# Fewer weight conversions in mid-attention, a row of -1 that stays in its tile, tail values split once per pair of heads

## The chip, the cores and the metric

The kernel runs on one core of one Trainium2 chip. The metric is the device time of one execution in microseconds (us), as the median of the runs shown. Five engines work beside each other on a core: TensorE (PE), VectorE (DVE), ScalarE (ACT), GpSimd (POOL) and SyncE (SP), which issues most of the DMAs.

## What is computed

```python
# 1: attention with rotary position, 4 batches x 8 heads, S = 576, D = 64
q_rot, k_rot = rotate(q), rotate(k)
attn = softmax(q_rot @ k_rot.T / 8)            # sums get +1e-9
x = (attn @ v)  ->  (4, 576, 512)
# 2: gated layer
u, v = split(gelu(x @ w_in));  v = layernorm(v) * g_ln
x = x + (u * (w_sg @ v + b_sg)) @ w_out
# 3: low-rank mixing of tokens, then two channel layers
u = x + (x.T @ U @ V).T
out = u + relu(u @ w_ch1) @ w_ch2
```

The weights w_in, U, V, w_out, w_ch1 and w_ch2 arrive as 64-bit floats in raw bits and are converted on the chip. Products in stages 2 and 3, and the scores, are made from a high and a low part of each number (high = the value rounded by a copy into the fp32r type, low = value minus high), so that three products stand for one.

## The kernel before, in words

**Attention** goes over 32 heads (two heads are a pair, 16 pairs) in slots. A head has five slots, one for each chunk c of its 576 keys (four of 128, a tail of 64). The main loop (lines 436 to 470) writes out by hand the order of all engines: in slot t = 5h + c PE makes the scores of head h, chunk c (`scores`, L244), ACT takes the exponent into a tile `pc` (L247), and three slots later PE multiplies by the values (`values`, L272). About thirteen slots ahead PE makes the same scores the other way round for the row maximum (`row_max`, L215), which DVE reduces (L220). These two kinds of score tile share three PSUM buffers ("ss"). Everything else is hung on a slot with `later(slot, fn)` and issued at the end of that slot; each engine then works through its own list in that order.

What is hung there for a head: the rotation, three POOL operations (`rope`, L147 to L149) at 26, 25 and 23 slots ahead; `high` (ACT copy L161 and one DMA) at 20 ahead; `low` (POOL subtraction L166 and two DMAs) at 17 ahead; and, at 11 ahead, a POOL memset (L172) that writes the row of -1 by which a row maximum is subtracted in the second score product. That row is row 64 of `K2`; `low` writes all 128 rows of `K2` and so wipes it each time. For the tail chunk, exponents are split (ACT L253, DVE `ph` L255) and so are the values: `value_stacks` has one ACT copy (L180) and one subtraction (L181; POOL, and DVE for the first two heads) for each head, in four tiles `VS`.

`finish` (L279 to L335) works once per pair at slot t0 = 10i + 12: the row sums are collected by two SP DMAs into `rc` (L303), at t0 + 5 POOL adds 1e-9 (`guard`, L306), at t0 + 7 DVE takes the reciprocal (L309), SP writes it to DRAM (L312, t0 + 8) and reads it back spread over rows (L317, t0 + 11), and DVE multiplies the two heads (`apply`, L324) at t0 + 24 and t0 + 26.

**Conversions** (`converted`, L337 to L343) are hung in the same slots. A chunk is a DMA into `raw64` (two buffers), 15 slots later ACT L71, DVE L72 to L75 in four successive slots, then an ACT copy (L349) and a POOL subtraction (L350) for the high and low part. There are eleven chunks, ten slots apart: eight of w_in (128 x 512) computed from slots 30, 40 ... 100, U (128 x 160) from 110, two halves of V (128 x 288) from 120 and 130. `t64` has one buffer.

**After attention** PE's order alone is written by hand; a list scheduler with a timeline of its own orders the other engines. The gated layer's first products (`v_step`, weights WVH and WVL) come first, then `u_step` (WUH, WUL), then the mixing by w_sg, whose rows come by DMA into two buffers `g` and are split by ACT (L516) and POOL (L506). Memory of the attention pool is reused by these tiles.

Of the kernel before, what the change touches and what calls it, by code (L numbers as in the profile page):

```python
# [29 lines left out]

LEAD = 26, 25, 23, 20, 17, 11
LEAD_IN = (-20, -19, -19, -8, -8, 1), (-19, -18, -16, -3, -1, 4), (-3, -3, 0, 2, 4, 8)
FIRST = (-17, -10), (-9, -9)

BY_ACT = (0, 1, 1, 1, 1), (1, 1, 0, 1, 1), (1, 0, 1, 1, 1)

LOAD, LOAD_V, SPLIT_V, SPLIT_V_FIRST = 30, 11, (6, 1), (-11, -1)


AHEAD, RAMP_FROM, RAMP, MAX_1, ROW, ROW_0, ROW_1 = 12, -1, 25, -1, 2, -8, -9

INVERSE = 5, 7, 8, 11, (24, 26)

MATRIX, APART, CONVERT, ROWS = 15, 10, 15, (151, 159)


IDLE = 17, 2, 5, 0, 2, 5, 6, 1, 0, 1
# [3 lines left out]
def tile_kernel(ctx: ExitStack, tc: tile.TileContext, qk, vv, tabs, w_in, g_ln, wsgT, b_sg, w_out, u_r, v_r, w1, w2, out):  # L53
# [32 lines left out]
    D = 64  # L86
# [45 lines left out]

    SPLITS = list(range(NC))[SPLIT]
    VSs = [p1.tile([P, 2, len(SPLITS), D + 1], F32R, name=f"VS_{i}") for i in range(4)]

    def load(h):
        nc.sync.dma_start(RAW[h % NR], qk[h // NHEAD, h % NHEAD].rearrange("c p s -> p c s"))
# [14 lines left out]
    def stacks(h, ticks):  # L152

        rot = RAW[h % NR][:, 0]
        K1, Q1, K2, Q2 = (t[h % NS] for t in (K1s, Q1s, K2s, Q2s))
        a, z = slice(0, D), slice(D, P)

        def high():  # L160
            nc.scalar.activation(K1, rot, AF.Copy)  # L161
            both = f(Qs[h % NS][a, :2 * S]).rearrange("p (a s) -> p a s", a=2)
            nc.sync.dma_start(both, f(K1[z]).rearrange("p (a s) -> p a s", a=1).to_broadcast([D, 2, S]))

        def low():
            nc.gpsimd.tensor_tensor(K2, rot, f(K1), ALU.subtract)  # L166
            nc.sync.dma_start(f(Q1[z]), f(K2[z]))
            nc.sync.dma_start(f(K1[z]), f(K1[a]))
        if h < len(BY_ACT):
            steps = rope(nc.gpsimd, h) + first_stacks(h)  # L170
        else:
            steps = rope(nc.gpsimd, h) + (high, low, lambda: nc.gpsimd.memset(f(K2[D:D + 1]), -1.0))  # L172
            value_stacks(h)
        for tick, fn in zip(ticks, steps):
            later(tick, fn)

    def value_stacks(h):
        VS = VSs[h % 4]
        src = VVs[(h // 2) % 3][:, SPLIT, h % 2, :D]
        later(max(NC * h - SPLIT_V[0], SPLIT_V_FIRST[0]), lambda: nc.scalar.activation(VS[:, 0, :, :D], src, AF.Copy))  # L180
        later(max(NC * h - SPLIT_V[1], SPLIT_V_FIRST[1]), lambda: (nc.gpsimd if h > 1 else nc.vector).tensor_tensor(VS[:, 1, :, :D], src, f(VS[:, 0, :, :D]), ALU.subtract))  # L181

    def first_stacks(h):

        rot = RAW[h % NR][:, 0]
        K1, Q1, K2, Q2 = (t[h % NS] for t in (K1s, Q1s, K2s, Q2s))
        a, z = slice(0, D), slice(D, P)

        def copy(on_act, out, x):
            if on_act:  # L190
                nc.scalar.activation(out, x, AF.Copy)  # L191
            else:
                nc.vector.tensor_copy(out, x)

        def high():
            e = BY_ACT[h]
            copy(e[0], Q1[z], rot[z])
            copy(e[1], Q1[a], rot[z])
            copy(e[2], K1[a], rot[a])
            copy(e[3], K1[z], rot[a])  # L200
            copy(e[4], Q2[a, 0:S], rot[z])

        def low():
            nc.vector.tensor_tensor(Q1[z], rot[z], f(Q1[z]), ALU.subtract)
            nc.vector.tensor_tensor(K2[a], rot[a], f(K1[a]), ALU.subtract)
        value_stacks(h)
        return high, low

# [28 lines left out]
    def scores(h, c):  # L237
        kk = TS[c]
        K1, Q1, K2, Q2 = (t[h % NS] for t in (K1s, Q1s, K2s, Q2s))
        ps = psp.tile([P, 2, 512], F32, tag="ss", name=f"st{h}_{c}", bufs=3)  # L240
        for l, r, st in ((K1, Q1, True), (K2[0:D + 1], Q2, False)):
# [12 lines left out]
        PCS[h, c] = ph  # L254
        lows.append(lambda: nc.vector.tensor_tensor(ph[D:], pt, f(ph[:D]), ALU.subtract))  # L255

    def values(h, c, t0):
        if c == 0:
            PVS[h] = psp.tile([P, 2, 512], F32, tag="pv", name=f"pv{h}", bufs=1)
        kk = TS[c]  # L260
        pc = PCS.pop((h, c))
        for n in range(2):
            ns = slice(n * HALF, (n + 1) * HALF)
            o = PVS[h][:D + 1, n, :HALF]
            if c in SPLITS:
# [13 lines left out]
    def finish(h, t0):  # L279
# [73 lines left out]
    def u_chunk(t0):
# [516 lines left out]
def _layout(q, k, v, moe_w_in, moe_g_ln, moe_w_sg, moe_b_sg, moe_w_out, moe2_U, moe2_V, moe2_w_ch1, moe2_w_ch2):  # L870
# [44 lines left out]
```

## Time and profile before

| | |
|---|---|
| median of 3 runs | 956.35 us (955.83 to 956.82) |
| the profiled execution's own time | 957.72 us |
| its span, first to last instruction | 955.9 us |
| mean granted TensorE clock | 0.989 of full speed |
| PE busy | 927.9 us (97%) |
| DVE, ACT, POOL busy | 542.5, 346.8, 409.9 us |

The span is cut into stretches below. A busy PE is not a PE at its peak, since matmuls are pipelined; so the pace in attention is read from the distance between equal events of successive heads. A line number is a line of the kernel before; `x2` means that two instructions are shown as one row.

### The profile page before, as it was taken

The page shows a single profiled execution, that of the slowest core. Times are in us where ns is not written, and L with a number is a line of the kernel's source. Part 1 is how long each engine was busy: PE and PEld are TensorE (multiplying, and loading weights), DVE is VectorE, ACT ScalarE, POOL GpSimd, SP SyncE. Part 2 cuts the span into 40 slices and gives each one's busy share as a digit, 9 for nine tenths or more (in the row PEclk, how much of TensorE's full clock was granted, in tenths as well). Part 3 has the DMA queues.
Part 4 walks back from the last instruction along what each step waited for, and adds up shares of the span by engine and source line. Part 5 has one row for each costly group of instructions (what it writes and reads, how often), then busy time and mean ns, then how long its engine had stood idle before and what let it go on. Part 6 is the DMA issues. An engine that isn't in the chain of part 4 may idle for free.

```text
span 955.9 us, 13163 instructions
## 1 busy us (share of the span) xinstructions
PE 927.9 (97%) x5179; PEld 784.5 (82%) x5180; DVE 542.5 (57%) x721; ACT 346.8 (36%) x550; POOL 409.9 (43%) x352
## 2 busy tenths in 40 slices
PE   5899999999999999999999899999999999999998
PEld 2588777777887888999999787888888888888887
DVE  7766899999874486334338845642642552222222
ACT  4356666666656443313225322311220320101000
POOL 7787999999943485231417533210210220000000
PEclk7899999999999999999999999999999999999999
DMA  5477776776630500000003001320220210000112
GB/s 176 127 206 201 210 206 182 207 191 173 168 90 14 164 25 1 1 1 19 5 23 111 22 23 46 109 67 1 88 88 1 67 45 0 1 1 23 45 48 86
DMA packets 57301, 77.93 MB, mean 82 GB/s; under 512 B 29756, under 2 KB 33111, under 8 KB 57239
## 3 DMA queue, kind: packets, MB, share of 16 engines
q1 hardware_dynamic: 56928, 77.01, 28.7%
q8 instruction: 41, 0.67, 0.3%
q14 instruction: 22, 0.17, 0.1%
q10 hardware_dynamic: 310, 0.08, 0.0%
HBM read 55.02 MB, written 4.79 MB: 63 GB/s over the span
## 4 chain that ended last, share of the span: by engine, by line
PE 74%; DVE 17%; issue 3%; DMA 2%; POOL 2%; ACT 1%; SPq 0%; ACTq 0%; DVEq 0%; POOLq 0%
PE a L542 21%; PE r L542 20%; PE pv L272 10%; PE st L244 6%; PE w L542 5%; DVE MX L220 4%; PE m L542 3%; PE sm L215 3%; PE u L542 3%; PE v L542 3%; DVE ph L255 2%; DVE t L74 1%; DVE t L72 1%; DVE X L324 1%; DVE t L75 1%
## 5 line engine op out<-in xcount | busy, mean ns | idle before, releaser
L272 PE MATMUL pv<-pc,VV 128*65 128x288 f32 x512 | 144.7, 405 | 0.5 <-DVE sums L293 0.5
L220 DVE TENSOR_REDUCE MX<-sm 128x1 f32<-128x576 f32 (+1 forms) x160 | 117.6, 751 | 36.5 <-PE sm L215 33.6
L244 PE MATMUL st<-Q,K 65*128 65x288 f32 (+3 forms) x640 | 126.5, 320 | 1.6 <-DVE MX L220 1.2
L735 DVE SCALAR_TENSOR_TENSOR RL<-r,RH 128x1024 fp32r<-128x1024 f32 (+1 forms) x38 | 42.3, 1112 | 123.8 <-ACT RH L734 123.7
L734 ACT ACTIVATE RH<-r 128x1024 fp32r<-128x1024 f32 (+1 forms) x38 | 35.6, 936 | 207.2 <-PE r L542 207.2
L244 PEld LDWEIGHTS st<-Q,K 65*128 65x128 f32 (+3 forms) x640 | 95.6, 179 | 16.2 <-DVE MX L220 5.4
L750 DVE TENSOR_TENSOR X<-a,X 128x256 f32<-128x256 f32 (+4 forms) x65 | 46.4, 745 | 90.8 <-PE a L542 90.7
L247 ACT ACTIVATE pc<-st 128x576 f32<-128x576 f32 x128 | 82.8, 648 | 36.5 <-PE st L244 31.1
L542 PE MATMUL a<-RH,setB 128*128 128x512 f32 (+1 forms) x320 | 93.3, 368 | 0.0
L272 PEld LDWEIGHTS pv<-pc,VV 128*65 128x65 f32 x512 | 68.5, 136 | 29.5 <-DVE sums L293 0.7
L215 PE MATMUL sm<-K,Q 128*128 128x288 f32 (+1 forms) x320 | 76.8, 325 | 12.8 <-ACT Q L191 6.9
L542 PE MATMUL a<-RH,setA 128*128 128x512 f32 (+1 forms) x288 | 83.8, 367 | 0.0
L542 PE MATMUL r<-UH,setA 128*128 128x512 f32 (+1 forms) x256 | 73.1, 364 | 0.1
L542 PE MATMUL r<-UH,setB 128*128 128x512 f32 (+1 forms) x256 | 73.2, 363 | 0.0
L215 PEld LDWEIGHTS sm<-K,Q 128*128 128x128 f32 (+1 forms) x320 | 52.5, 184 | 20.2 <-ACT Q L191 7.4
L542 PEld LDWEIGHTS a<-RH,setB 128*128 128x128 f32 x320 | 58.2, 189 | 10.0
L506 POOL TENSOR_TENSOR setB<-t,setB 128x512 fp32r<-128x512 f32 x16 | 20.7, 1294 | 102.9 <-ACT setB L695 91.8
L542 PEld LDWEIGHTS a<-RH,setA 128*128 128x128 f32 x288 | 52.1, 188 | 9.0
L542 PE MATMUL a<-RL,setB 128*128 128x512 f32 (+1 forms) x160 | 58.9, 368 | 0.0
L148 POOL TENSOR_TENSOR raw<-raw,tab 128x576 f32<-128x576 f32 x31 | 54.5, 1760 | 5.6 <-DMA raw<-in_qk 5.6
L506 POOL TENSOR_TENSOR setA<-t,setA 128x512 fp32r<-128x512 f32 x16 | 21.5, 1352 | 73.7 <-ACT setA L695 69.9
L542 PEld LDWEIGHTS r<-UH,setA 128*128 128x128 f32 x256 | 46.1, 188 | 8.2 <-DVE X L676 0.4
(170 smaller groups left out, 2030.3 us busy)
## 6 DMA issues: line engine op xcount, KB each, us to landing
raw<-in_qk SPq DMA_DIRECT2D x31, 576.0 KB, 4.8
raw<-in_w SPq DMA_DIRECT2D x24, 512.0 KB, 3.6
Q<-K SPq DMA_DIRECT2D x29, 288.0 KB, 3.5
VV<-in_vv SPq DMA_DIRECT2D x16, 320.0 KB, 3.9
rb<-rr SPq DMA_DIRECT2D x15, 288.0 KB, 3.7
Q<-K SPq DMA_DIRECT2D x29, 144.0 KB, 2.4
K<-K SPq DMA_DIRECT2D x29, 144.0 KB, 2.4
raw<-in_w_in SPq DMA_DIRECT2D x8, 512.0 KB
```

The lines of the kernel that those rows point to most:

```text
L148: lambda: e.tensor_tensor(raw[:, 1], raw[:, 1], tab[:, 1], ALU.mult),
L215: nc.tensor.matmul(ps[:TS[t], n, :HALF], Q1[:, t * P:t * P + TS[t]], K1[:, n * HALF:(n + 1) * HALF], start=True, stop=True)
L220: nc.vector.tensor_reduce(MXs[h % 2][:TS[t], t:t + 1], ps[:TS[t], :, :HALF], AX.XY, ALU.max)
L244: nc.tensor.matmul(ps[:kk, n, :HALF], l[:, c * P:c * P + kk], r[:, ns], start=st, stop=not st)
L247: nc.scalar.activation(h2(pc[:kk]), ps[:kk, :, :HALF], AF.Exp, scale=0.125)
L255: lows.append(lambda: nc.vector.tensor_tensor(ph[D:], pt, f(ph[:D]), ALU.subtract))
L272: nc.tensor.matmul(o, l, r, start=(c == 0 and j == 0), stop=(c == NC - 1 and j == len(pr) - 1))
L506: return nc.gpsimd.tensor_tensor(out, a, b, ALU.subtract)
L542: nc.tensor.matmul(o, l, rr, start=(j == 0), stop=(j == n - 1))
L734: nc.scalar.activation(RH[:, s], ps[:, :, :WIDE[blk]], AF.Relu)
L735: nc.vector.scalar_tensor_tensor(RL[:, s], ps[:, :, :WIDE[blk]], 0.0, f(RH[:, s]), ALU.max, ALU.subtract)
L750: nc.vector.tensor_tensor(X[b][:, e2, xs], ps[:, :n, us], X[b][:, e2, xs], ALU.add)
```

## The change

1. **Conversions.** U from slot 40, the first half of V from 80 and the second from 115; two chunks of w_in from 60 and 100; the other six from 125, 132, 139, 146, 153 and 160. The DMA is issued 8 slots ahead of the first five and 6 slots ahead of the six. The four chunks for `v_step` come before the four for `u_step`.
2. **The row of -1.** Queries and keys change places in the tiles: ACT's copy goes to `Q1`, its DMA to the halves `K1` and `K2` of one tile (64 rows each), POOL's subtraction to `Q2`, whose row 64 is overwritten by the row maximum later in any case. `K2` is 65 rows high; nothing writes its last row after the first time. The memset stays for the first use of each of the five buffers only.
3. **Tail values** are split once per pair (128 columns instead of 64), in two tiles.
4. **The guard** (+1e-9) moves from POOL at t0 + 5 to DVE at t0 + 7, right ahead of the reciprocal.

```diff
-LEAD = 26, 25, 23, 20, 17, 11
+LEAD = 26, 25, 23, 20, 17
-INVERSE = 5, 7, 8, 11, (24, 26)
+INVERSE = 7, 8, 11, (24, 26)
-MATRIX, APART, CONVERT, ROWS = 15, 10, 15, (151, 159)
+MATRIX, SMALL, ROWS = ((60, 8), (100, 8)) + tuple((t, 6) for t in range(125, 165, 7)), ((40, 8), (80, 8), (115, 8)), (151, 159)
...
-    K1s = [p1.tile([P, S], F32R, name=f"K1_{i}") for i in range(NS)]
-    Qs = [p1.tile([P, S + NC * P], F32R, name=f"Q_{i}") for i in range(NS)]
-    Q1s = [t[:, :S] for t in Qs]
-    Q2s = [t[:D + 1, S:] for t in Qs]
-    K2s = [p1.tile([P, S], F32R, name=f"K2_{i}") for i in range(NS)]
+    Q1s = [p1.tile([P, S], F32R, name=f"Q1_{i}") for i in range(NS)]
+    Ks = [p1.tile([P, 2 * S], F32R, name=f"K_{i}") for i in range(NS)]
+    K1s = [t[:, :S] for t in Ks]
+    K2s = [t[:D + 1, S:] for t in Ks]
+    Q2s = [p1.tile([P, NC * P], F32R, name=f"Q2_{i}") for i in range(NS)]
...
         def high():
-            nc.scalar.activation(K1, rot, AF.Copy)
-            both = f(Qs[h % NS][a, :2 * S]).rearrange("p (a s) -> p a s", a=2)
-            nc.sync.dma_start(both, f(K1[z]).rearrange("p (a s) -> p a s", a=1).to_broadcast([D, 2, S]))
+            nc.scalar.activation(Q1, rot, AF.Copy)
+            both = f(Ks[h % NS][a]).rearrange("p (a s) -> p a s", a=2)
+            nc.sync.dma_start(both, f(Q1[z]).rearrange("p (a s) -> p a s", a=1).to_broadcast([D, 2, S]))
 
         def low():
-            nc.gpsimd.tensor_tensor(K2, rot, f(K1), ALU.subtract)
-            nc.sync.dma_start(f(Q1[z]), f(K2[z]))
-            nc.sync.dma_start(f(K1[z]), f(K1[a]))
+            nc.gpsimd.tensor_tensor(Q2[:, :S], rot, f(Q1), ALU.subtract)
+            nc.sync.dma_start(f(K1[z]), f(Q2[z, :S]))
+            nc.sync.dma_start(f(Q1[z]), f(Q1[a]))
...
-            steps = rope(nc.gpsimd, h) + (high, low, lambda: nc.gpsimd.memset(f(K2[D:D + 1]), -1.0))
+            steps = rope(nc.gpsimd, h) + (high, low)
+            if h < NS:
+                steps += lambda: nc.gpsimd.memset(f(K2[D:]), -1.0),
...
     def value_stacks(h):
-        VS = VSs[h % 4]
-        src = VVs[(h // 2) % 3][:, SPLIT, h % 2, :D]
+        if h % 2:
+            return
+        VS = VSs[h // 2 % 2]
+        src = VVs[(h // 2) % 3][:, SPLITS[0], :, :D]
...
-        def guard():
-            nc.gpsimd.tensor_scalar_add(rc, rc, 1e-9)
-
         def invert():
+            nc.vector.tensor_scalar_add(rc, rc, 1e-9)
             nc.vector.reciprocal(rc, rc)
...
-    WTICK = [MATRIX + APART * i for i in range(2 * KT + 3)]
-    for i in range(2 * KT):
-        w_in_chunk(WTICK[i], i)
-    u_chunk(WTICK[2 * KT])
-    for a in range(2):
-        v_chunk(WTICK[2 * KT + 1 + a], a)
+    u_chunk(SMALL[0])
+    w_in_chunk(MATRIX[0], 0, 1)
+    v_chunk(SMALL[1], 0)
+    w_in_chunk(MATRIX[1], 1, 1)
+    v_chunk(SMALL[2], 1)
+    for i in range(2, 2 * KT):
+        w_in_chunk(MATRIX[i], i % KT, i < KT)
...
-    x = [t.transpose(0, 1, 3, 2) for t in (k, q)]
+    x = [t.transpose(0, 1, 3, 2) for t in (q, k)]
```

## Rows read from the trace of the kernel before

**Rows 1.** The page: busy time of each engine, share of the span, instructions

```profile
PE 927.9 (97%) x5179; PEld 784.5 (82%) x5180; DVE 542.5 (57%) x721; ACT 346.8 (36%) x550; POOL 409.9 (43%) x352
```

**Rows 2.** The chain that ended last: start us, us, what (attention)

```profile
104.00 1.50 PE pv L272 x8
...
129.29 1.86 DVE ph L255
...
147.16 1.87 DVE ph L255
...
229.02 1.50 PE pv L272 x8
...
288.40 1.49 PE pv L272 x8
```

**Rows 3.** Stretches: length, busy time of each engine (instructions), clock, DMA share, GB/s

```profile
78.00:95.00 17.00, 17.00 (x105) 13.86 (x104) 11.59 (x20) 11.13 (x20) 11.73 (x11) 1.00 0.84 210
...
130.40:148.30 17.90, 17.67 (x104) 13.75 (x103) 17.71 (x22) 11.53 (x21) 17.38 (x15) 1.00 0.75 198
...
237.00:254.00 17.00, 17.00 (x104) 13.86 (x104) 14.38 (x22) 11.39 (x22) 15.80 (x14) 1.00 0.74 195
...
288.00:305.00 17.00, 17.00 (x101) 13.35 (x100) 6.93 (x9) 11.90 (x21) 5.68 (x5) 1.00 0.07 19
```

**Rows 4.** Line L71, the first operation of the eleven chunks

```profile
L71 ACT ACTIVATE t<-raw x11: 347/655/667, 86.2 to 262.1; 128x512 f32<-128x512 f32 x8, 128x288 f32<-128x288 f32 x2, 128x160 f32<-128x160 f32 x1
```

**Rows 5.** Timeline of DVE: start, us, line, operation (three stretches, the second crowded)

```profile
104.73 0.42 DVE L72 TENSOR_SCALAR t<-t 128x512 f32<-128x512 f32 x1
...
137.41 0.19 DVE L309 RECIPROCAL rc<-rc 128x9 f32<-128x9 f32 x1
137.63 1.79 DVE L255 TENSOR_TENSOR ph<-pt,ph 64x576 fp32r<-64x576 f32 x1
139.45 1.42 DVE L220 TENSOR_REDUCE MX<-sm 128x1 f32<-128x576 f32 x2
140.79 1.69 DVE L72 TENSOR_SCALAR t<-t 128x512 f32<-128x512 f32 x1
...
242.40 0.75 DVE L324 TENSOR_TENSOR X<-stage,rb 64x576 f32<-64x576 f32 x1
```

**Rows 6.** Groups by line and shape: count | busy us, mean ns | idle before

```profile
L148 POOL TENSOR_TENSOR raw<-raw,tab 128x576 f32<-128x576 f32 x31 | 54.5, 1760 | 5.6 <-DMA raw<-in_qk 5.6
...
L172 POOL MEMSET K<- 1x576 f32 x29 | 16.7, 578 | 1.7
L181 POOL TENSOR_TENSOR VS<-VV,VS 128x64 fp32r<-128x64 f32 x30 | 15.4, 512 | 11.9 <-ACT VS L180 11.9
...
L306 POOL TENSOR_SCALAR rc<-rc 128x9 f32<-128x9 f32 x16 | 8.0, 502 | 17.9 <-DMA rc<-sums 6.5 <-PE sm L215 5.4 <-DMA rc<-stage 4.9
```

**Rows 7.** Stretches, instructions on a chunk's tile `t` alone, columns as in rows 3

```profile
130.40:148.30 17.90, 0.00 (x0) 0.00 (x0) 4.38 (x4) 1.29 (x2) 1.79 (x1) 1.00 0.75 198
237.00:254.00 17.00, 0.00 (x0) 0.00 (x0) 3.83 (x4) 1.44 (x4) 0.53 (x1) 1.00 0.74 195
```

**Rows 8.** The DMA issues: line, count, size, median us to landing

```profile
rc<-stage SPq DMA_DIRECT2D x30, 2.2 KB, 3.0
```

**Rows 9.** The chain again, a chunk's load and the turn to the gated layer

```profile
185.59 4.52 DMA raw<-in_w_in
...
313.08 4.39 DMA rb<-rr
...
319.68 4.85 DMA g<-in_wsgT
```

**Rows 10.** Timeline of POOL and PE where attention ends

```profile
306.27 1.66 POOL L419 TENSOR_TENSOR XL<-X,XH 128x576 fp32r<-128x576 f32 x1 [0.77 <-ACT XH L416]
...
341.81 0.53 PE L542 MATMUL m<-WSH,VH 128*128 128x288 f32 x2 [1.01 <-ACT WSH L516]
343.34 0.54 PE L542 MATMUL m<-WSL,VH 128*128 128x288 f32 x2 [1.01 <-POOL WSL L506]
```

More of the change, by code (lines that the diff above doesn't have):

```diff
@@ L27 @@
 SPLIT = slice(4, 5)
-LEAD = 26, 25, 23, 20, 17, 11
-LEAD_IN = (-20, -19, -19, -8, -8, 1), (-19, -18, -16, -3, -1, 4), (-3, -3, 0, 2, 4, 8)
+LEAD = 26, 25, 23, 20, 17
+LEAD_IN = (-20, -19, -19, -8, -8), (-19, -18, -16, -3, -1, 4), (-3, -3, 0, 2, 4, 8)
 FIRST = (-17, -10), (-9, -9)
 BY_ACT = (0, 1, 1, 1, 1), (1, 1, 0, 1, 1), (1, 0, 1, 1, 1)
-LOAD, LOAD_V, SPLIT_V, SPLIT_V_FIRST = 30, 11, (6, 1), (-11, -1)
+LOAD, LOAD_V, SPLIT_V = 30, 11, (6, 1)
 AHEAD, RAMP_FROM, RAMP, MAX_1, ROW, ROW_0, ROW_1 = 12, -1, 25, -1, 2, -8, -9
-INVERSE = 5, 7, 8, 11, (24, 26)
-MATRIX, APART, CONVERT, ROWS = 15, 10, 15, (151, 159)
+INVERSE = 7, 8, 11, (24, 26)
+MATRIX, SMALL, ROWS = ((60, 8), (100, 8)) + tuple((t, 6) for t in range(125, 165, 7)), ((40, 8), (80, 8), (115, 8)), (151, 159)
 IDLE = 17, 2, 5, 0, 2, 5, 6, 1, 0, 1
@@ L133, in tile_kernel @@
     SPLITS = list(range(NC))[SPLIT]
-    VSs = [p1.tile([P, 2, len(SPLITS), D + 1], F32R, name=f"VS_{i}") for i in range(4)]
+    VSs = [p1.tile([P, 2, 2, D + 1], F32R, name=f"VS_{i}") for i in range(2)]
     def load(h):
@@ L177, in value_stacks @@
     def value_stacks(h):
-        VS = VSs[h % 4]
-        src = VVs[(h // 2) % 3][:, SPLIT, h % 2, :D]
-        later(max(NC * h - SPLIT_V[0], SPLIT_V_FIRST[0]), lambda: nc.scalar.activation(VS[:, 0, :, :D], src, AF.Copy))
-        later(max(NC * h - SPLIT_V[1], SPLIT_V_FIRST[1]), lambda: (nc.gpsimd if h > 1 else nc.vector).tensor_tensor(VS[:, 1, :, :D], src, f(VS[:, 0, :, :D]), ALU.subtract))
+        if h % 2:
+            return
+        VS = VSs[h // 2 % 2]
+        src = VVs[(h // 2) % 3][:, SPLITS[0], :, :D]
+        later(NC * h - SPLIT_V[0], lambda: nc.scalar.activation(VS[:, 0, :, :D], src, AF.Copy))
+        later(NC * h - SPLIT_V[1], lambda: (nc.gpsimd if h else nc.vector).tensor_tensor(VS[:, 1, :, :D], src, f(VS[:, 0, :, :D]), ALU.subtract))
     def first_stacks(h):
@@ L196, in high @@
             e = BY_ACT[h]
[L197 to L201, printed above, removed]
+            copy(e[0], K1[z], rot[z])
+            copy(e[1], K1[a], rot[z])
+            copy(e[2], Q1[a], rot[a])
+            copy(e[3], Q1[z], rot[a])
+            copy(e[4], K2[a], rot[z])
         def low():
-            nc.vector.tensor_tensor(Q1[z], rot[z], f(Q1[z]), ALU.subtract)
-            nc.vector.tensor_tensor(K2[a], rot[a], f(K1[a]), ALU.subtract)
+            nc.vector.tensor_tensor(K1[z], rot[z], f(K1[z]), ALU.subtract)
+            nc.vector.tensor_tensor(Q2[a, :S], rot[a], f(Q1[a]), ALU.subtract)
         value_stacks(h)
@@ L240, in scores @@
         ps = psp.tile([P, 2, 512], F32, tag="ss", name=f"st{h}_{c}", bufs=3)
-        for l, r, st in ((K1, Q1, True), (K2[0:D + 1], Q2, False)):
+        for l, r, st in ((K1, Q1, True), (K2, Q2[:D + 1], False)):
             for n in range(2):
@@ L265, in values @@
             if c in SPLITS:
-                VS = VSs[h % 4]
-                j = SPLITS.index(c)
-                pr = [(VS[:, 0, j], pc[:, ns]), (VS[:, 1, j], pc[:, ns])]
+                VS = VSs[h // 2 % 2]
+                pr = [(VS[:, 0, h % 2], pc[:, ns]), (VS[:, 1, h % 2], pc[:, ns])]
             else:
@@ L328, in finish @@
         later(t0, collect)
-        for tick, fn in zip(INVERSE, (guard, invert, gather, spread)):
+        for tick, fn in zip(INVERSE, (invert, gather, spread)):
             later(t0 + tick, fn)
@@ L332, in finish, with converted, w_in_chunk @@
             for a in range(2):
-                later(t0 + (INVERSE[4][a] if i < NP - 2 else 16 + a), lambda a=a: apply(a))
+                later(t0 + (INVERSE[3][a] if i < NP - 2 else 16 + a), lambda a=a: apply(a))
         else:
             later(t0 + 16, apply_last)
-    def converted(t0, src, n, use):
+    def converted(at, src, n, use):
         raw = p1.tile([P, 512, 2], U32, tag="raw64", name="raw64", bufs=2)[:, :n]
         t = p1.tile([P, 512], F32, tag="t64", name="t64", bufs=1)[:, :n]
-        later(t0, lambda: nc.sync.dma_start(raw.rearrange("p n w -> p (n w)"), src))
+        later(at[0] - at[1], lambda: nc.sync.dma_start(raw.rearrange("p n w -> p (n w)"), src))
         for j, fn in enumerate(from_f64(t, raw) + use(t)):
-            later(t0 + CONVERT + j, fn)
-    def w_in_chunk(t0, i):
-        k, c = divmod(i, DFF // 512)
+            later(at[0] + j, fn)
+    def w_in_chunk(at, k, c):
         hi, lo = SETA[2 * c][:, k], SETA[2 * c + 1][:, k]
-        converted(t0, w_in[k * P:(k + 1) * P, c * 1024:(c + 1) * 1024], 512, lambda t: (
+        converted(at, w_in[k * P:(k + 1) * P, c * 1024:(c + 1) * 1024], 512, lambda t: (
             lambda: nc.scalar.activation(hi, t, AF.Copy),
@@ L351, in w_in_chunk, with u_chunk @@
         ))
-    def u_chunk(t0):
+    def u_chunk(at):
         def use(t):
@@ L358, in use, with v_chunk @@
             )
-        converted(t0, u_r, NC * 32, use)
-    def v_chunk(t0, a):
+        converted(at, u_r, NC * 32, use)
+    def v_chunk(at, a):
         hs = slice(a * HALF, (a + 1) * HALF)
-        converted(t0, v_r[:, 2 * a * HALF:2 * (a + 1) * HALF], HALF, lambda t: (
+        converted(at, v_r[:, 2 * a * HALF:2 * (a + 1) * HALF], HALF, lambda t: (
             lambda: nc.scalar.activation(V4[:, hs], t, AF.Copy),
@@ L386, in tile_kernel @@
     for i in range(len(BY_ACT)):
-        nc.gpsimd.memset(f(K2s[i][D:D + 1]), -1.0)
+        nc.gpsimd.memset(f(K2s[i][D:]), -1.0)
     for i in range(3):
@@ L391, in tile_kernel @@
         nc.gpsimd.memset(MXs[i], 0.0)
-    for i in range(4):
+    for i in range(2):
         nc.gpsimd.memset(f(VSs[i][:, 0, :, D:]), 1.0)
```

## The prediction

> **What bounds the kernel now.** The page comes first: PE is busy for 97% of the span [rows 1], so only stretches where PE runs below its own pace can give anything. In attention that pace is read from the chain, at the same step of successive heads. From 229.02 to 288.40 lie 59.38 us, seven heads at 8.48 us. From 104.00 to 229.02 lie 125.02 us, and two `ph` steps two heads apart stand 17.87 us apart (129.29, 147.16) [rows 2]; so these are fourteen heads, at 8.93 us each. Fourteen at 8.48 would take 118.76 us: **6.26 us** are lost there, 0.89 us a pair.
>
> The stretches say to whom. At 130.4 to 148.3 both DVE (17.71 of 17.90 us) and POOL (17.38) are full; at 237 to 254, with DVE at 14.38 and POOL at 15.80 of 17.00, PE keeps its pace [rows 3]. The loss lies within the time of the eleven chunks, 86.2 to 262.1 us, one per pair [rows 4], and ends where the eight large ones have been done and the small ones follow. The very first chunk, at 86 to 95 us, costs PE nothing, since POOL has only 11.73 of 17.00 us to do there [rows 3].
>
> Why two engines are full at once is seen in DVE's own operations. L72 takes 0.42 us at one place and 1.69 at another; `ph` takes 1.79 where the like multiplication with two SBUF inputs takes 0.75 in the quieter stretch; the maximum, whose input is in PSUM, stays at 0.71 each [rows 5]. So some DVE work waits for POOL, in stretches where POOL never stops.
>
> The rest of the span, after about 311 us, does the same instructions as before; the change reaches it only through the time at which attention hands over.
>
> **The change, part by part.** The profiled execution took 957.72 us, 1.37 above the median of 956.35; its span of 955.9 leaves 1.82 us outside. I work in its time and take the result off the median.
>
> *POOL's load.* Per pair the memsets take 2 x 0.578 = 1.16 us, the value subtractions 2 x 0.512, the guard 0.50 [rows 6], a chunk's low part 1.79 [rows 7]. Gone or moved: 1.16; of the second nothing to the whole 1.02 less one operation, so 0 to 0.51 (128 columns at once are not in the trace; the nearest row is one of 64, whose 0.512 is mostly waiting, so I take 0.5); and 0.50. That is 2.2 us a pair with a chunk, 17.38 to about 15.2, and 4.0 less in one without. The one is below the 15.80 beside which PE kept its pace [rows 3], the other far below.
>
> *DVE's load.* A pair without a chunk loses L72 to L75, 4.38 us with their waits [rows 7], out of 17.71: 13.3 us, plus the guard, in 16.97. So the pairs without a chunk come back to 8.48 us a head, and the 6.26 us are the ceiling of the gain, since PE's own work is not touched.
>
> *Pairs that keep a large chunk* while POOL still rotates: slots 60, 100 and 125. Bounds: nothing (the pairs of the small chunks, which lost none with POOL at 15.80), and the 0.89 of now. DVE has 0.55 us more to do on a large chunk than on the small ones of 237 to 254 (4.38 against 3.83 [rows 7]), beside a POOL with 0.6 us less than there; I take 0.3 each, nearer to the zero, **+0.9 us**. U and the two halves of V cost nothing, as now.
>
> *The guard on DVE.* Nearest row: the reciprocal on the same 128 x 9 elements, 0.19 us [rows 5]; POOL's own mean is 0.50 [rows 6]. Bounds 0.19 and, if it waits like L72 (1.69 against 0.42), 0.2 + 1.3 = 1.5 us. In a pair without a chunk, 13.3 + 1.5 = 14.8 us still fit into 16.97, so it is hidden either way. The trace shows that the same operation type on large tiles waits for POOL and that the reciprocal does not. The Trainium skill, page "SBUF — State Buffer", section "Who interferes with whom", says that a tensor_scalar in a two-port mode and a GpSimd instruction exclude each other for a whole instruction; by it the guard would take the 1.5 us, and the sum would be the same except in the three chunk pairs, up to 0.9 us each.
>
> At the end the guard stands on the chain: rows read back at 313.08, then DVE, then the next `g` load at 319.68 [rows 9]. POOL is idle there, so **+0.2 us**. The wait for the collected sums comes onto DVE too: seven slots of 1.70 us, 11.9 us, lie between that DMA's slot and the guard, and it lands 3.0 us after issue [rows 8]. Queued behind it would be the row maxima, on which PE waits; covered.
>
> *DMAs and SP's queue.* Eleven chunk loads are issued as before, 8 slots of 1.70 us (13.6 us) or 6 slots (10.2 us, a little less where the row maxima have ended) ahead; one took 4.52 us [rows 9], so it lands in time. Six loads move behind the last head loads into a stretch with a DMA share of 0.07 [rows 3]. The stacks' DMAs are the same ones with other names. Cost: none; if SP is held up by more than some 5 us, ACT waits in L71, and behind it the exponents.
>
> *Six chunks in slots 125 to 166.* At 288 to 305 ACT is busy 11.90 of 17.00 us, DVE 6.93, POOL 5.68 [rows 3]. A chunk each seven slots (10.2 us) adds 1.29 us to ACT, so 2.2 us in this stretch (14.1 of 17.0), at most 4.38 to DVE and 1.79 to POOL [rows 7]. Row maxima end near slot 147, so little on DVE is urgent. ACT is the tight one near slot 153; the exponents have about two slots of room. Bounds 0 and 0.89 (what a crowded pair loses now); I take **+0.2 us**.
>
> *The hand-over.* POOL's four splits XL now stand behind the low part of the chunk of slot 153; each takes 1.66 us [rows 10]. So they end up to 1.8 us later against PE, which waits for none of them now, and could wait that long. PE waits twice for 1.01 us in the first mixing step [rows 10] for things that hang on the `g` loads, and would use that up first. The `t64` and `raw64` buffers are given back at slot 166 instead of 137, so tiles laid over them are written a little later; the next wait is for a `g` load that took 4.85 us [rows 9], which covers it. Cost taken: nothing; bounds 0 and 1.8, less than the two waits together.
>
> *Value copies on ACT* fall from 32 to 16, and 27 memsets go: off the path but for POOL's load above.
>
> **Sum:** -6.26 + 0.9 + 0.2 + 0.2 = -4.96 us. 957.72 becomes 952.8; off the median, 956.35 - 4.96 = **951.4 us**.
>
> **The rivals.** *(a) Contention stays where chunks stay.* The three large-chunk pairs keep their 0.89, the end costs its upper bound: -6.26 + 2.7 + 0.2 + 0.9 = -2.5, or 953.9. For it: DVE is over its pace with a full chunk as soon as each operation waits. Against: POOL gets 2 us of gaps a pair.
>
> *(b) The cost only moves.* Each of the six late chunks costs what one costs now, 0.89, through ACT's exponents or the late XL: 5.3 us, so -6.26 + 5.3 + 0.4 = -0.6, or 955.8. For it: ACT at 14 of 17 us in bursts. Against: no row maxima there, POOL two thirds idle.
>
> *(c) Slower: the guard's wait holds up DVE.* If SP issues the collecting DMAs more than 11.9 - 3.0 = 8.9 us late, DVE stands still with the maxima behind it, once per pair. It passes the old time when it costs over 4.96 / 15 = 0.33 us a pair; at 1 us a pair the time is 951.4 + 15 = 966. Against: on POOL, two slots earlier, this wait cost 4.9 us from the pairs' DMAs in all and 6.5 from the last pair's, each once, where POOL ran ahead [rows 6].
>
> That the changed parts do nothing at all is not among them: the removed instructions are in the trace.
>
> **How the numbers follow.** About 0.2%, 1.9 us, is what a measurement of this kernel can tell from no change: faster is below 954.4, slower above 958.3. My forecast has 0.72, (a) 0.15, (b) 0.08, (c) 0.05. The forecast's own range goes from 950.0 (the ceiling of 6.26 and no costs) to 953. For 8 in 10 the range reaches into (a): 949.8 to 954.2. Faster: 0.72 and most of (a), 0.84; same: the rest of (a) and (b), 0.12; slower 0.04.
>
> **What would show it.** Right: between the fourteen heads 8.48 us each where no chunk is; DVE and POOL both under 16 us in such a pair of 17; `ph` often near 0.75; 27 fewer memsets and no idle time of DVE at the guard; the end of attention some 5 us earlier and the turn to the second layer as long as now. Wrong: pairs at 17.9 us with POOL not full; DVE waiting for the collected sums; PE waiting for XL by more than its two waits now; a longer stretch from the last value product to the second layer.

## The result, and the profile after

| | before | after |
|---|---|---|
| median, runs side by side | 956.56 us (955.83 to 956.82, 4 runs) | 962.78 us (961.63 to 964.43, 4 runs) |
| the profiled execution's own time | 957.72 us | 964.43 us |
| its span | 955.9 us | 962.6 us |

The ratio is **1.0068** (95% interval 1.0048 to 1.0087): slower by 6.2 us, where 951.4 us had been forecast (range 949.8 to 954.2).

The page's busy time of the engines in the changed kernel answers to [rows 1]:

```profile
PE 933.2 (97%) x5179; PEld 786.5 (82%) x5180; DVE 534.9 (56%) x736; ACT 345.0 (36%) x534; POOL 372.6 (39%) x290
```

POOL does 37 us less and DVE 8 us less. The load was taken off as planned, and the kernel became slower. The chain says where (start, us, what; `pv ... x8` is the same step of successive heads):

```profile
44.42 1.50 PE pv L275 x8
...
148.50 1.50 PE pv L275 x8
...
156.86 1.80 DVE ph L259
166.74 1.49 PE pv L275 x8
...
290.75 1.50 PE pv L275 x8
...
305.28 1.51 PE pv L275 x8
...
374.77 10.39 PE w L543 x76
```

From 44.42 to 290.75 are 28 heads, 246.33 us. At the pace of 8.483 (59.38 us / 7, [rows 2]) they take 237.52, so attention now loses **8.8 us**. Three rows of the kernel before's chain answer to the first of these and to the last two:

```profile
44.62 1.50 PE pv L272 x8
...
302.90 1.51 PE pv L272 x8
...
370.00 10.41 PE w L542 x76
```

There the 28 heads go from 44.62 to 288.40 [rows 2] and lose 6.26 us. One pair here, 148.50 to 166.74, takes 18.24 us instead of 16.97. One stretch of [rows 3], and the pair behind it (columns as there), show that DVE and POOL aren't full in it:

```profile
130.40:148.30 17.90, 17.60 (x102) 13.49 (x101) 16.07 (x22) 11.22 (x20) 10.46 (x8) 1.00 0.73 168
148.30:166.20 17.90, 17.35 (x102) 13.31 (x101) 13.85 (x19) 10.36 (x17) 15.84 (x12) 1.00 0.69 186
```

From 148.3 to 166.2 DVE is busy for 13.85 us and has no operation of a chunk; POOL, 17.38 in the stretch before it in the old kernel [rows 3], has 15.84. By their sums both fit. What happens is seen in the order of single operations. DVE at the end of a pair, then POOL, ACT and PE at the same moment (all of the changed kernel's timeline):

```profile
137.76 0.15 DVE L309 TENSOR_SCALAR rc<-rc 128x9 f32<-128x9 f32 x1
137.95 0.21 DVE L310 RECIPROCAL rc<-rc 128x9 f32<-128x9 f32 x1
138.19 2.00 DVE L259 TENSOR_TENSOR ph<-pt,ph 64x576 fp32r<-64x576 f32 x1
...
138.15 1.42 POOL L166 TENSOR_TENSOR Q<-raw,Q 128x576 fp32r<-128x576 f32 x1 [1.91 <-ACT Q L161]
...
137.40 0.67 ACT L161 ACTIVATE Q<-raw 128x576 fp32r<-128x576 f32 x1
...
140.24 0.74 PE L275 MATMUL pv<-ph,VS 128*65 128x288 f32 x4 [0.26 <-DVE ph L259]
```

The guard (L309) takes 0.15 us here and waits for nothing. But `ph` behind it starts at 138.19, **0.04 us after** POOL's subtraction at 138.15, and takes 2.00 us where 0.75 does [rows 5]. PE waits for it. Without the guard's 0.2 us `ph` would have been first. And it comes again: in every second pair POOL is idle ahead of that subtraction, waiting for ACT's high copy, and so starts 0.75 us after that copy does, at the same place of PE's order. Two pairs later ACT's copy starts at 173.80, POOL at 174.55 and `ph` at 174.57, for 2.01 us. In the pairs between, as at 156.86 in the chain, the guard takes 0.39 us, and `ph` comes 0.23 us after POOL's third rotation (L149) and takes 1.80.

One pair between 96 and 240 us is free of this and shows what a late `ph` costs (PE, DVE, POOL, PE):

```profile
113.97 0.90 PE L275 MATMUL pv<-ph,VS 128*65 128x288 f32 x4
...
120.61 0.75 DVE L259 TENSOR_TENSOR ph<-pt,ph 64x576 fp32r<-64x576 f32 x1
...
121.17 1.46 POOL L166 TENSOR_TENSOR Q<-raw,Q 128x576 fp32r<-128x576 f32 x1 [0.88 <-ACT Q L161]
...
130.95 0.90 PE L275 MATMUL pv<-ph,VS 128*65 128x288 f32 x4
```

There `ph` is first by 0.56 us and takes 0.75, and the pair from 113.97 to 130.95 takes 16.98 us, the full pace, with the guard in its place. The other seven pairs of that stretch take 17.76 to 18.25 us by the same measure and lose 7.7 of the 8.8 us. What PE's weight loads waited for between 95 and 240 us (us in total, times, longest) says the same:

```profile
PEld pv L275 <- DVE ph L259: 5.4, 7, 0.8
...
PEld st L248 <- DVE MX L224: 2.8, 9, 0.3
```

These are seven waits for the seven late `ph`, and smaller ones for the row maxima that stand behind it on DVE. In the kernels of experiments 1, 2 and 9 neither row is there.

POOL's groups between 40 and 300 us show that it now waits for ACT, which it hardly did when it was full (6.2 us at L166 and 3.5 at L350 in the kernel before):

```profile
L166 POOL TENSOR_TENSOR Q<-raw,Q 128x576 fp32r<-128x576 f32 x28 | 41.7, 1490 | 34.4 <-ACT Q L161 34.3
...
L350 POOL TENSOR_TENSOR setA<-t,setA 128x512 fp32r<-128x512 f32 x6 | 8.1, 1348 | 36.1 <-ACT setA L349 36.1
```

**The clock.** The two profiled executions differ by 6.7 us. The later end of attention is 2.4 of them; most of the rest is this. Stretches of 2 us at the turn to the gated layer (columns as in [rows 3]; the third value from the end is the granted clock):

```profile
345.00:347.00 2.00, 1.00 (x4) 0.56 (x4) 1.93 (x5) 2.00 (x5) 0.47 (x1) 1.00 0.00 0
347.00:349.00 2.00, 0.99 (x7) 0.96 (x7) 2.00 (x2) 0.92 (x3) 2.00 (x2) 0.91 0.00 0
349.00:351.00 2.00, 2.00 (x10) 2.00 (x10) 2.00 (x2) 1.21 (x3) 2.00 (x3) 0.50 0.00 0
351.00:353.00 2.00, 2.00 (x14) 2.00 (x13) 2.00 (x2) 0.00 (x0) 2.00 (x3) 0.74 0.00 0
```

The like stretches at one place of the kernel before:

```profile
546.00:548.00 2.00, 2.00 (x13) 2.00 (x12) 1.75 (x3) 1.28 (x2) 1.16 (x1) 0.65 0.00 0
548.00:550.00 2.00, 2.00 (x10) 2.00 (x10) 0.00 (x0) 0.00 (x0) 2.00 (x1) 0.50 0.03 8
```

After PE had been busy for only half of 345 to 349 (three waits of 0.37, 1.00 and 1.01 us in the first mixing step), the granted clock goes from 1.00 to 0.50 of full speed, 2.4 to 1.2 GHz, and back. What is lost is 2 x (0.09 + 0.50 + 0.26) = **1.7 us** of PE's time, an estimate and at most that, since PE is not full in all of it. The kernel before shows one such fall in its profiled execution between the first 44 us and PE's last product, the changed one three (here, from 536.4 and from 553.4). So of 6.7 us, two falls more are 3.4, the end of attention (305.28 against 302.90) is 2.4, and 0.9 are left for all the rest. In the other three runs of the changed kernel the mean granted clock is 0.989 to 0.990, that of the profiled one 0.986 and of the kernel before 0.989: falls are not what makes those slower. How their 5 to 7 us divide isn't seen, for want of a trace.

### The profile page after: what moved, and what is told of

Read it like the earlier page. It is cut to its first block, busy times and chain, and to the rows that moved or that the text cites. A ratio compares the mean times of both kernels' runs of the same rounds, so it can differ in the third digit from the quotient of the medians.

```text
span 962.6 us, 12973 instructions
## 1 busy us (share of the span) xinstructions
PE 933.2 (97%) x5179; PEld 786.5 (82%) x5180; DVE 534.9 (56%) x736; ACT 345.0 (36%) x534; POOL 372.6 (39%) x290
## 4 chain that ended last, share of the span: by engine, by line
PE 80%; DVE 11%; DMA 3%; issue 2%; ACT 1%; POOL 1%; SPq 0%; ACTq 0%; POOLq 0%; DVEq 0%
PE a L543 21%; PE r L543 20%; PE pv L275 11%; PE st L248 8%; PE w L543 5%; PE m L543 4%; PE v L543 4%; PE sm L219 3%; PE u L543 3%; DVE MX L224 2%; DVE ph L259 1%; DMA Q<-Q 1%; DVE g L624 1%; DVE t L74 1%; PE t L647 1%
## 5 line engine op out<-in xcount | busy, mean ns | idle before, releaser
L166 POOL TENSOR_TENSOR Q<-raw,Q 128x576 fp32r<-128x576 f32 x29 | 43.6, 1504 | 34.4 <-ACT Q L161 34.3
L543 PE MATMUL a<-RL,setA 128*128 128x512 f32 (+1 forms) x144 | 52.7, 366 | 0.0
```

The lines of the kernel that those rows point to most:

```text
L166: nc.gpsimd.tensor_tensor(Q2[:, :S], rot, f(Q1), ALU.subtract)
L543: nc.tensor.matmul(o, l, rr, start=(j == 0), stop=(j == n - 1))
```

## The experiments

All change the changed kernel but one. In the table, "attention" is what the 28 heads lose against 237.52 us, `ph` its mean between 95 and 290 us, "falls" the falls of the clock between 44 us and PE's last product, and the last column but one the span less 1.7 us for each; all from the profiled executions. Ratios are to the kernel before on the same chip; the rows are from different chips, so they are compared by their ratios and intervals, and rows whose intervals overlap are not told apart.

| kernel | attention, us | `ph`, ns | falls | span less falls | ratio, 95% interval |
|---|---|---|---|---|---|
| before | 6.3 | 1500 | 1 | 954.2 | |
| after | 8.8 | 1140 | 3 | 957.5 | 1.0068 [1.0048, 1.0087] |
| 1 guard on POOL | 2.0 | 788 | 1 | 951.3 | 0.9986 [0.9974, 0.9998] |
| 2 inverse early | 3.9 | 852 | 1 | 950.4 | 0.9985 [0.9974, 0.9996] |
| 3 chunks as before | 12.7 | 1198 | 1 | 959.8 | 1.0074 [1.0053, 1.0095] |
| 4 before, guard on DVE | 4.6 | 1231 | 1 | 951.9 | 0.9990 [0.9978, 1.0002] |
| 5 second reciprocal | 7.0 | 1226 | 1 | 959.7 | 1.0070 [1.0055, 1.0085] |
| 6 inverse early, chunks sooner | 5.4 | 959 | 1 | 952.2 | 0.9969 [0.9957, 0.9981] |
| 7 memsets back | 7.3 | 1235 | 1 | 958.3 | 1.0048 [1.0035, 1.0062] |
| 8 tail values per head | 5.0 | 973 | 2 | 953.7 | 1.0016 [1.0007, 1.0025] |
| 9 inverse behind `ph` | 3.0 | 851 | 2 | 952.4 | 1.0031 [1.0020, 1.0042] |
| 10 as 6, values per head | 5.3 | 1048 | 1 | 951.8 | 0.9992 [0.9983, 1.0001] |
| 11 as 1, chunks sooner | 3.9 | 941 | 0 | 952.5 | 1.0008 [0.9999, 1.0016] |
| 12 as 1, all earlier | 1.9 | 773 | 1 | 952.8 | 1.0001 [0.9989, 1.0012] |

### 1 and 2: the guard on POOL again; the inverse early

```diff
-INVERSE = 7, 8, 11, (24, 26)
+INVERSE = 5, 7, 8, 11, (24, 26)
...
+        def guard():
+            nc.gpsimd.tensor_scalar_add(rc, rc, 1e-9)
...
         def invert():
-            nc.vector.tensor_scalar_add(rc, rc, 1e-9)
...
```
```diff
-INVERSE = 7, 8, 11, (24, 26)
+INVERSE = 5, 8, 11, (24, 26)
```

> The changed kernel with the guard back on POOL at slot t0 + 5. Theory G (the guard, 0.15 to 0.4 us on DVE just ahead of the tail subtraction ph, lets POOL's low start first, so that ph waits a whole POOL operation at the end of every second head; 2.00 us instead of 0.75 with POOL starting 0.04 us earlier): most of the 8.8 us lost in attention come back, 957 to 958 us, ph near 0.75 us after the reciprocal. Rival P (POOL now runs in one dense burst per head, released by ACT's high copy, and DVE's multiplications fall into it wherever the guard stands): not more than 1 us comes back, 961.5 to 963. Rival S (the moved conversions alone cost it): no change, 962.5 to 963.

> The changed kernel with guard and reciprocal both on DVE at slot t0 + 5 instead of t0 + 7, so that nothing of them stands ahead of ph at the end of the pair. Theory G: as with the guard on POOL or 0.5 us better, 956.5 to 958 us. Rival P: within 1 us of the changed kernel, 961.5 to 963. If DVE's wait for the collected sums matters, it shows here, with two slots less of lead: DVE idle at L309.

955.03 and 954.63 us, both below what theory G gave (957 to 958 and 956.5 to 958). The place of the one instruction per pair is worth some 8 us (ratio 1.0068 to 0.9986). The first kernel's DVE and POOL at a pair's end:

```profile
154.04 0.77 DVE L259 TENSOR_TENSOR ph<-pt,ph 64x576 fp32r<-64x576 f32 x1
...
154.16 1.92 POOL L148 TENSOR_TENSOR raw<-raw,tab 128x576 f32<-128x576 f32 x1
```

Now `ph` starts 0.12 us ahead of POOL, and POOL's operation is the one that takes longer. In the second kernel the guard itself waits for POOL, at a place where nobody waits for DVE (its group on DVE, 95 to 290 us):

```profile
L309 DVE TENSOR_SCALAR rc<-rc 128x9 f32<-128x9 f32 x12 | 12.2, 1020 | 0.0
```

Its mean is 1.02 us there against 0.24 in the changed kernel, and the kernel is 8 us faster. So it isn't the guard's own duration that costs.

### 3: the chunks where they were

```diff
...
+    for i in range(2 * KT):
+        w_in_chunk((30 + 10 * i, 15), *divmod(i, 2))
+    u_chunk((110, 15))
+    for a in range(2):
+        v_chunk((120 + 10 * a, 15), a)
```

> The changed kernel with the conversions at their old slots (30, 40 ... 130, loads 15 slots ahead), all else as changed. Theory G: the loss in attention stays, since the guard stays, at 0.9 us a pair or more over fourteen heads and now also over the late ones; only the hand-over comes back by 2 us: 960 to 961. Rival S (the moved conversions cost it): at or below the kernel before, 950 to 956. Rival P: the old chunks fill POOL's gaps and set its phase: attention as before, 956 to 957.

963.05 us, above the 960 to 961 of theory G. With the other three parts alone attention loses 12.7 us, so moving the chunks is worth 3.9 there; it isn't what made the kernel slow. POOL's group (95 to 290 us) shows it standing still for a chunk's copy, about 4 us each time, instead of being ahead:

```profile
L350 POOL TENSOR_TENSOR setA<-t,setA 128x512 fp32r<-128x512 f32 x8 | 10.2, 1273 | 32.1 <-ACT setA L349 32.1
```

### 4: the kernel before, with the guard on DVE

```diff
-INVERSE = 5, 7, 8, 11, (24, 26)
+INVERSE = 7, 8, 11, (24, 26)
...
         def invert():
+            nc.vector.tensor_scalar_add(rc, rc, 1e-9)
...
```

> The kernel before with only the guard moved to DVE ahead of the reciprocal. Theory G: ph loses to POOL also in the late pairs that were free (229 to 288 us, three and a half pairs at up to 0.9 us), and the full pairs get 0.2 us each: 958.5 to 961. Rivals P and S: 956.3 to 957.

955.24 us, where theory G had 958.5 to 961: it missed. The same move costs nothing here. In the kernel before `ph` waits for POOL nearly always (mean 1500 ns), so in the full pairs there is no start left to lose, and POOL is relieved of its 0.50 us (mean 1231). In the late pairs, which had been free, seven heads lose 0.45 us in all (226.10 to 285.93, 59.83 us against 59.38). So the guard ahead of `ph` isn't slow by itself; it depends on what POOL starts at that moment.

### 5: a second reciprocal in the guard's place

```diff
...
+    spare = keep.tile([P, 16], F32, name="spare")
...
+        def guard():
+            nc.gpsimd.tensor_scalar_add(rc, rc, 1e-9)
...
         def invert():
-            nc.vector.tensor_scalar_add(rc, rc, 1e-9)
+            nc.vector.reciprocal(spare[:, :2 * S // P], rc)
...
```

> The kernel with the guard back on POOL (955.0 us), and on DVE a second reciprocal of the same 128 x 9 elements, written to a spare tile, right ahead of the first: 0.2 us of DVE time, no wait on POOL, no sums waited for that were not waited for anyway. Theory T (it is the time ahead of ph that decides the race with POOL's next operation): most of the loss is back, 959 to 962 us, ph after the reciprocal at 1.7 to 2.0 us. Theory L (the guard hurts because a tensor_scalar itself waits for POOL and holds DVE): 955 to 956, ph near 0.75.

963.28 us, above the 959 to 962 of theory T. The second reciprocal is additional work whose result isn't used. DVE and POOL at a pair's end, and one of DVE's groups:

```profile
154.75 0.19 DVE L313 RECIPROCAL spare<-rc 128x9 f32<-128x9 f32 x1
154.98 0.21 DVE L314 RECIPROCAL rc<-rc 128x9 f32<-128x9 f32 x1
155.22 1.90 DVE L259 TENSOR_TENSOR ph<-pt,ph 64x576 fp32r<-64x576 f32 x1
...
155.10 1.41 POOL L148 TENSOR_TENSOR raw<-raw,tab 128x576 f32<-128x576 f32 x1
```

```profile
L313 DVE RECIPROCAL spare<-rc 128x9 f32<-128x9 f32 x11 | 2.1, 193 | 0.0
```

An operation that never waits (193 ns in the mean) brings the loss in attention from 2.0 back to 7.0 us. Not all of the 8 us of total time is this: from its row at 547.90 to the end the run takes 3.3 us longer than the kernel before from 545.70 (413.5 against 410.2), where the chain's products of the last layer take 5.60 us each beside 5.49 (603.33 here, 600.73 there). No other run's end is longer by as much. The spare tile lies in memory that lives to the end; that its place shifts others is a guess that wasn't tried.

### 6, 10 and 11: the six late chunks sooner

```diff
-((60, 8), (100, 8)) + tuple((t, 6) for t in range(125, 165, 7))
+((60, 8), (100, 8)) + tuple((t, 6) for t in range(122, 158, 6))
```

Number 6 adds this to 2, number 11 to 1, and number 10 to 2 together with the tail values per head (8 below).

> The kernel with guard and reciprocal at t0 + 5 (954.6 us), and the six late chunks at slots 122, 128 ... 152 instead of 125, 132 ... 160, so that the last one is done before attention ends. Theory H (the last chunk's operations stand in DVE's, ACT's and POOL's queues ahead of the hand-over's): the hand-over, 66.0 us from the last full head to the second batch's w products, gets 1 to 2 us shorter, 952.5 to 953.7. Rival (the hand-over hangs on the chain of row sums and g loads alone): no change, 954.3 to 955. If ACT is too dense with chunks six slots apart, attention gets longer by up to 1 us.

> The changed kernel with the inverse early, the six late chunks in slots 122 to 152 and the tail values split per head again, as before the change. Theory T: splitting per head helped by 3 to 4 us only because it moved ph ahead of GpSimd's next operation; with the inverse early there is little of that left to win, so the time stays within 1.5 us of the version with values per pair (954.3): 953 to 956. Rival V (the split per pair costs in itself, by waits of its own on ScalarE and GpSimd): the two gains add up, 954.3 - 3.5 = 950 to 952 us.

> The changed kernel with the guard on GpSimd at slot 5 (as before the change) and the six late chunks in slots 122 to 152. If the sooner chunks take 1 to 2 us off the hand-over whatever the attention does: with the guard on GpSimd 955.0 becomes 953 to 954.5 us, the hand-over near 66 instead of 67.5, and the loss in attention 2 to 3.5 us. If the sooner chunks only give back in attention what the hand-over gains: 954.5 to 956 us.

954.30, 954.11 and 955.64 us. Number 6 has the best ratio of all, 0.9969, and beats both kernels. But what the sooner chunks add is not settled: its interval touches that of 2, its trace loses 1.5 us more in attention, and on top of 1 the same step gives nothing (0.9986 to 1.0008, attention 2.0 to 3.9 us): about half of this lies between 250 and 269 us, where the sooner chunks meet the last rotations; the other half lies between 197 and 216 us, where numbers 1 and 11 have the same work, and wasn't followed. Splitting the values per head adds nothing to an early inverse, as the first of its two expectations has it; by the ratios (0.9992 against 0.9969) number 10 is even the slower.

### 7 and 8: the memsets back; the tail values per head

```diff
...
-            if h < NS:
-                steps += lambda: nc.gpsimd.memset(f(K2[D:]), -1.0),
+            steps += lambda: nc.gpsimd.memset(f(K2[D:]), -1.0),
```
```diff
...
-        src = VVs[(h // 2) % 3][:, SPLITS[0], :, :D]
-        later(NC * h - SPLIT_V[0], lambda: nc.scalar.activation(VS[:, 0, :, :D], src, AF.Copy))
+        src = VVs[(h // 2) % 3][:, SPLITS[0], h % 2, :D]
+        later(NC * h - SPLIT_V[0], lambda: nc.scalar.activation(VS[:, 0, h % 2, :D], src, AF.Copy))
...
```

> The changed kernel with the memset of the row of -1 issued for every head again, at its old place, 11 slots ahead (it writes the same value into a row that holds it). Theory I (the guard costs that much only because POOL, with less to do, idles at fixed waits and packs its rotations into the slots in which DVE has its multiplications, guard, reciprocal and ph in a row; the memsets take up that slack): faster than the changed kernel although work is added, 956 to 959 us, POOL's waits for ACT in attention down from 80 us by a third or more. Rival (the memsets were only load): 963 to 965.

> The changed kernel with the tail values split once per head again (two operations of 64 columns at their old slots, in the changed tiles). Theory I: as with the memset but with half of its load, 958 to 962 us. Rival (load only): 963 to 964.

961.82 and 958.60 us, the first above what was expected if slack on POOL were what helps. Giving POOL back the 1.16 us a pair of its memsets changes little; giving it back two small operations for one takes 4 to 5 us off (1.0068 to 1.0016). Both add load and neither is slower, so the load is not the cause. Between 95 and 240 us PE's weight loads wait for `ph` five times in number 7 and four times in number 8, against seven. In number 8 `ph` at 172.70 starts 0.12 us ahead of POOL's subtraction at 172.82 and takes 0.75. Why just this moves the phase was not followed further.

### 9: the inverse just behind `ph`

```diff
-INVERSE = 7, 8, 11, (24, 26)
+INVERSE = 8, 9, 12, (24, 26)
```

> The changed kernel with one number set of slots altered: the guard and the reciprocal go from slot 7 after a pair's end to slot 8 (and the two DMAs behind them one slot later), so that VectorE does them just behind the exponents' remainder ph instead of just ahead of it. The work is the same, engine by engine. Theory T (the order at the pair's end decides: what stands ahead of ph makes it start behind GpSimd's next operation): the loss in attention falls from 8.8 to between 2 and 5 us, as in the run with the inverse early, and the time is 954 to 957 us. Rival L (the guard costs what it costs wherever VectorE does it, while the early place helped for another reason, such as the wait for the row maxima there): 961 to 963 us, the loss in attention stays at 8 to 9.

957.63 us, so 0.9963 of the changed kernel (1.0031 / 1.0068), a little above what was expected; two falls of the clock lie in the profiled execution. The instructions and their engines are the same, only their order is another; the two DMAs of the reciprocal come one slot later with it. The timeline of the pair shown for the changed kernel (DVE, then POOL, ACT), and DVE's groups:

```profile
136.78 0.75 DVE L259 TENSOR_TENSOR ph<-pt,ph 64x576 fp32r<-64x576 f32 x1
...
138.24 0.60 DVE L309 TENSOR_SCALAR rc<-rc 128x9 f32<-128x9 f32 x1
...
137.07 1.74 POOL L166 TENSOR_TENSOR Q<-raw,Q 128x576 fp32r<-128x576 f32 x1 [1.91 <-ACT Q L161]
...
136.31 0.67 ACT L161 ACTIVATE Q<-raw 128x576 fp32r<-128x576 f32 x1
```

```profile
L259 DVE TENSOR_TENSOR ph<-pt,ph 64x576 fp32r<-64x576 f32 x22 | 18.7, 851 | 0.9
L309 DVE TENSOR_SCALAR rc<-rc 128x9 f32<-128x9 f32 x11 | 6.1, 558 | 0.0
```

POOL again waits 1.91 us for ACT and again starts 0.76 us after ACT's copy does. But `ph`, with nothing ahead of it, is 0.29 us earlier than POOL and takes 0.75 us. Now it is the guard that waits, 0.56 us in the mean instead of 0.24, and nobody minds. Attention loses 3.0 us instead of 8.8. That shows the cause of the loss in attention with no instruction added, taken off or moved to another engine. The time follows in part: 0.9963 is 3.6 us for 5.8 in attention, and where the other 2 go isn't seen.

### 12: as 1, with guard and reciprocal earlier still

```diff
-INVERSE = 5, 7, 8, 11, (24, 26)
+INVERSE = 4, 6, 8, 11, (24, 26)
...
-            nc.gpsimd.tensor_scalar_add(rc, rc, 1e-9)
+            (nc.gpsimd if i < NP - 1 else nc.vector).tensor_scalar_add(rc, rc, 1e-9)
```

> The changed kernel with the guard on GpSimd at slot 4 for all pairs but the last, whose guard is VectorE's, and the reciprocal on VectorE at slot 6 for all, so that nothing but the row maxima stands ahead of ph, and neither guard nor reciprocal stands behind the last chunk at the hand-over. Theory T: the loss in attention is that of the run with the guard on GpSimd or less (2 us or less) and the hand-over that of the run with the inverse early (66 instead of 67.5), so the ratio to the kernel before is 0.995 to 0.998, below the 0.9986 of the guard on GpSimd at slot 5. Rival P (which pairs lose their order is a matter of the phase that the rest of the work happens to have, and any shift can win or lose as much as this gains): a loss of 3 to 5 us and a ratio of 0.998 to 1.001. If GpSimd comes late with the guard, VectorE shows idle time at the reciprocal.

956.73 us, 1.0001. Attention is the best of all (1.9 us lost), as theory T has it, but the ratio is that of rival P; its interval overlaps with that of 1. Its chain:

```profile
283.52 1.50 PE pv L275 x8
...
298.03 1.52 PE pv L275 x8
...
343.20 3.75 DVE t L74 x2
...
366.98 11.71 PE w L545 x76
```

Attention ends 4.9 us earlier than before (298.03 against 302.90), and the gated layer's `w` row starts only 3.0 us earlier (366.98; 370.00 in the kernel before). Between them the chain runs over DVE's conversions for the next layer, whose L74 starts at 343.20 here and at 343.90 in the kernel before.

## Why the prediction was wrong

**Busy time was the wrong measure.** "The pairs without a chunk come back to 8.48 us a head" is the step that failed, and in it the sentence on the guard, "14.8 us still fit into 16.97, so it is hidden either way". DVE is busy for 13.85 us in the stretch of such a pair and POOL for 15.84, 1.27 of it for a chunk; over the two pairs from 149.09 to 185.35 us POOL has 13.7 us each, chunk included, where 13.4 without one had been forecast. So both loads came as forecast, and the pair takes 18.24; pairs of 17.9 us with POOL not full are the first of the prediction's own signs of being wrong. PE waits for `ph` within its head; what counts is when `ph` starts. 0.2 to 0.4 us ahead of it put it behind an operation of POOL of 1.4 us, in seven pairs of eight. The prediction left attention 1.1 us of loss; 8.8 were measured. That is 7.7 of the 11.6 us between its 952.8 and the 964.43 of the profiled execution; two more falls of the clock are 3.4. The Trainium skill, page "SBUF — State Buffer", section "Who interferes with whom", says that "Issue order, not op shape, decides who blocks." The traces agree: `ph` takes 0.77 us when it is first by 0.12 (number 1) and 2.00 when it is last by 0.04 (the changed kernel). The prediction had weighed that section for how long the guard would wait, and not for what the guard makes wait.

**What of it was right.** The loss of 6.26 us was mostly DVE waiting for POOL, and 4.3 of it could be won: with the guard on POOL (1 and 12), attention loses 1.9 to 2.0 us, where 1.1 was forecast (0.9 for three chunk pairs, 0.2 at the end). The guard's own duration at that place was 0.15 us, or 0.39 to 0.41 in the pairs in which it waits, within its bounds. There is no idle time of DVE ahead of it (0.0 in its groups), so the rival in which it waits for the collected sums did not come; the kernel got slower by something no rival named.

**The hand-over, taken at 0 (bounds 0 to 1.8).** From the last head's first value product to the gated layer's `w` row it took 69.49 us (305.28 to 374.77) against 67.10; 1.7 of these 2.4 are the fall of the clock. PE's waits before it are those the prediction asked for:

```profile
315.86 0.50 PE L543 MATMUL v<-setA,XL 128*128 128x512 f32 x1 [0.28 <-POOL XL L420]
317.42 0.50 PE L543 MATMUL v<-setA,XL 128*128 128x512 f32 x1 [0.58 <-POOL XL L420]
```

0.86 us for XL, within the bound, but the two waits of 1.01 us [rows 10] were not used up: they came again, behind a third of 0.37. And the last chunk stands on DVE ahead of the guard:

```profile
317.95 0.69 DVE L75 SCALAR_TENSOR_TENSOR t<-raw,t 128x512 uint32<-128x512 uint32 x1
318.56 4.54 DVE L325 TENSOR_TENSOR X<-stage,rb 64x576 f32<-64x576 f32 x4
323.13 0.60 DVE L309 TENSOR_SCALAR rc<-rc 128x9 f32<-128x9 f32 x1
```

Guard and reciprocal wait for L75 and four multiplications, which the prediction took for uncritical at the end. With the inverse early (2) three of these multiplications come behind it: the guard starts 14.1 us after the last head's first value product (314.14, 300.06) instead of 17.9, and the `w` row follows that product after 65.97 us.

**What could not have come.** Even with attention near its forecast, 951.4 was not reached: the runs that lose least there (1 and 12) are at 0.9986 and 1.0001. Part of an earlier end is given back in the gated layer (12), which the prediction took over whole. In number 1 little is: attention ends 4.1 us earlier than in the kernel before's trace, its `w` row comes 3.8 earlier (366.24) and its span is 2.9 shorter, and yet the medians on that chip (955.03 and 956.23) differ by 1.2. The profiled execution of the kernel before, from which the 6.26 us were read, was 1.4 us above its median; whether its other executions lose less in attention isn't known, for want of a trace.

**Open.** Why this layout puts `ph` and POOL within 0.04 to 0.23 us of each other is seen (both follow ACT and PE), but not why the tail values per pair do it and the memsets hardly. Nor how the 6.2 us between the medians divide.

## What to carry to other kernels

Busy time per stage says whether work fits, not whether it is on time. Before an operation is put on an engine's list, look which one stands behind it there, who waits for that, and what on the other engine starts at the same moment; here 0.2 us at the wrong place took attention's loss from 2.0 to 8.8 us, and one place further down the list to 3.0. A relieved engine doesn't only get gaps: here POOL began to wait for ACT, and then its starts came in step with the very work that they collide with.

## What the hardware showed that was not expected

- A wait between DVE and POOL is decided by starts 0.04 to 0.3 us apart, and the late one waits until the other's operation ends (`ph` 0.75 to 2.01 us, POOL's L147 1.94 instead of 1.42). The reciprocal (0.19 to 0.22 us everywhere) never waits; the guard on the same 128 x 9 elements takes 0.15 when it is free and 1.02 in the mean at slot 5.
- The granted clock of TensorE fell after PE had waited, in the gated layer (from 341 to 367 us) and at the turn behind it (from 530 to 553 us), and each fall cost up to 1.7 us; but not each wait was followed by one. The changed kernel, its three falls told above, and number 11 stand at the ends: there PE waits the same 2.48 us as the kernel before at the same `w` step, and no fall follows.

```profile
543.36 0.52 PE L545 MATMUL w<-GH,WOH 128*128 128x288 f32 x2 [2.48 <-DVE VL L738]
```

So two profiled executions of this kernel may differ by several us without any difference in the program, and spans were compared here with the falls taken off.
